# Attention and two feed-forwards: 768 plain and 1024 Strassen tokens instead of 896 and 896

## The chip, the cores and the metric

The kernel runs on one core of a Trainium2 chip. The metric is the device time of one execution in microseconds (us). PE is the tensor engine (matmul), PEld its weight loads, DVE the vector engine, ACT the scalar engine, POOL GpSimd, SP the engine that issues most DMAs.

## The reference

Multi-head attention with head mixing before and after the softmax, then two feed-forwards on the attention's output x (4 x 448 = 1792 tokens of 768):

```
scores = einsum('bhij,hg->bgij', q @ k.T / 8, w_pre)         # 4 batches, 12 heads, 448 x 448
attn   = softmax(scores); attn = einsum('bhij,hg->bgij', attn, w_post)
x      = attn @ v                                            # 1792 x 768
x      = (x @ w1) * (x @ w2) @ w3 @ w_out                    # 768 -> 1024 -> 1024 -> 768
h      = x @ w_in;  out = max(0.01 h, h) @ w_out2            # 768 -> 2048 -> 768
```

The inputs q, k, v are float32, the weights of the feed-forwards float64. The output is float32.

## The kernel before

Every product of the feed-forwards is made as three matmuls: each operand is split into a high part (rounded by ACT's copy, `hi_act`, L71) and a low part (the rest, by a DVE subtraction, `lo_dve`, L74), and high x high, high x low and low x high are added in PSUM. Weights arrive as 64-bit words and are converted on the chip (`converting`, L94): one copy on ACT (L99), four operations on DVE (L100 to L110), then the split. Three raw blocks can be in flight.

**Attention** (L117) is ordered by hand. Scores are made in chunks of 120, 120, 120 and 88 query columns; `pq` (L210) are the scores, evicted as `s`, rearranged by DMAs into `sr`, mixed across heads by `pm` (L277, premix), then softmax (`mx`, `e`, `sm`), weighing (`weigh`, L308 on ACT and L310 on POOL), `po` (L331, postmix), transposes `ap` on DVE, and `px` (L363), the product with v (`vs`). A table gives the step in which loads are issued; `at(max(g0//2-1, 2), "v", b)` (L449) loads batch 0's v in step 2, from ACT's queue. The result is stored in DRAM as `scr`: batches 0 and 1 already split into high and low, batches 2 and 3 whole.

**The drain.** While the last chunk of attention runs down, `seam()` (a generator in `first_half`) is advanced at fixed places: it loads x of the first 896 tokens (L711), converts the first w1 block and lets PE make the first 36 products `pm` (L541).

**First half** (`first_half`, L585): 896 tokens by plain products, 512 + 384 wide (`PARTS`). For each of 8 blocks of 128 hidden columns one w1 and one w2 product, beside which w_out and w3 are converted; then the fold (`pw`, L613: w3 times w_out, kept in DRAM as w34); then w34 and the w_in blocks (`pm`), and `second_product` (`po`, L555) with w_out2, in groups of FQ=4 w_in blocks.

**Second half** (`second_half`, L807): the other 896 tokens as two halves of 448, by a seven-product scheme of Strassen's kind (`seven`, L857; `pp`, L852) for w1/w2 and w_in, w34 by plain products, and `second_product` again. Converted blocks come back from DRAM (`kept_*`), sums of blocks from `sums_*`.

From the drain on, a scheduler that simulates the timeline sets the order of instructions on each engine. A DMA is issued on one of eight lanes (DMAHW0 to 7) taken in turn; it waits until the lane's earlier DMA has landed, and the issuing queue runs in order.

Of the kernel before, what the change touches and what calls it, by code (L numbers as in the profile page):

```python
# [8 lines left out]
F32 = mybir.dt.float32  # L9
# [13 lines left out]
def attention_moe_kernel(ctx: ExitStack, tc, qt, kt, vt, w_pre, w_post, w1, w2, w3t, w_out, w_in2, w_out2, out):  # L23
# [27 lines left out]
    while i0 < S:  # L51
# [4 lines left out]
    scr = [  # L56
        dram.tile([2, P, NPAIR, S], F32, name=f"scr_{b}") if b < 2 else dram.tile([P, NPAIR, S], F32, name=f"scr_{b}")
        for b in range(B)
    ]
# [57 lines left out]
    def attention(seam):  # L117
        with ExitStack() as es, ExitStack() as left:
# [229 lines left out]
            def av(b, c, p):  # L348
# [21 lines left out]
                def out():  # L370
                    hi, lo = (y[:, i, 2 * g:2 * g + 2, :ni] for i in range(2))
                    if b < 2:
                        hi_act(hi, px[:, :, :ni])
                    nc.scalar.copy(lo.bitcast(F32), px[:, :, :ni])
                    if b < 2:
                        nc.gpsimd.tensor_tensor(out=lo, in0=lo.bitcast(F32), in1=hi.bitcast(F32), op=ALU.subtract)
# [3 lines left out]
                if p == NPAIR - 1:  # L380
                    if b < 2:
                        later.extend((scr[b][i, :, :, c0:c0 + ni], y[:, i, :, :ni].bitcast(F32)) for i in range(2))
                    else:
                        later.append((scr[b][:, :, c0:c0 + ni], y[:, 1, :, :ni].bitcast(F32)))
# [132 lines left out]
    def moe():  # L517
        KM, KF, KF2 = DM // P, DF // P, DF2 // P
        T = 2 * S
        NT = T // P  # L520
# [3 lines left out]
        PARTS = ((0, 512), (512, T - 512))  # L524
# [21 lines left out]
        def second_product(g, wts, acc, s, f, beside=iter(())):  # L546

            for t in range(NT):
                for hf in range(2):
# [3 lines left out]
                    for m in range(FQ):  # L553
                        for j, (a, c) in enumerate(TERMS):
                            nc.tensor.matmul(  # L555
                                po, g[m][:, a, t * P:(t + 1) * P], wts[m][:, c, cs],
                                start=(m == 0 and j == 0), stop=(m == FQ - 1 and j == 2),
# [5 lines left out]
                if f + FQ == KF2:  # L563
                    r0 = s * T + t * P
                    nc.sync.dma_start(out=out[r0:r0 + P, :], in_=acc[:, t, :])
# [19 lines left out]
        def first_half():  # L585
            with ExitStack() as er:
# [4 lines left out]
                def wo_parts(kk):  # L591
# [5 lines left out]
                    if kk == 4:  # L597
                        t = ap.tile([P, NT, DM], F32R, tag="acc", name="wo")
                        extra = ap.tile([P, DM], F32R, tag="wx", name="wo")
                        for i in range(4, KF):  # L600
                            wos[i] = t[:, 2 * i - 8], (t[:, 2 * i - 7] if i < KF - 1 else extra)
# [97 lines left out]
                def seam():  # L699
# [42 lines left out]
                h0 = pool(es, "m_h0")  # L742
                xx = [x[:, kk] for kk in range(KM)]
# [37 lines left out]
                acc = ap.tile([P, NT, DM], F32, tag="acc", name="acc")  # L781
# [25 lines left out]
        def second_half():  # L807

            with ExitStack() as es:
# [3 lines left out]
                HALF = ((0, S), (S, S))  # L813

                def operand(name):
                    t = xo.tile([P, KH, 2, S], F32R, tag="xo", name=name, bufs=7)
# [31 lines left out]
                def product(w, i, b):  # L848
                    dst = bank([P, S], "pp")
# [8 lines left out]
                def seven(w, b, put_block):  # L858
# [3 lines left out]
                    def partial(tag, x, y):  # L862
                        u = tm.tile([P, S], F32, tag=tag, name=tag)
                        tt(u, x, y, ALU.add)
                        return u

                    x1 = product(w, A11, b11)
                    p1 = tm.tile([P, S], F32, tag="p1", name="p1")
                    nc.scalar.activation(out=p1, in_=x1, func=ACTF.Copy)
                    x5 = product(w, S1, t1)  # L870
                    put_block(0, 0, product(w, A12, b21), p1)
# [3 lines left out]
                    put_block(1, 1, x5, u3)  # L875
                    put_block(1, 0, product(w, A22, t4), u3)
# [199 lines left out]
```

## Time and profile before

| | us |
|---|---|
| runs (three) | 1226.17, 1231.8, 1974.27; median 1231.8 |
| profiled execution | 1224.22, span 1222.4 |
| PE busy | 1207.7 (99%) |
| DVE busy | 866.5 (71%) |
| ACT busy | 532.7 (44%) |
| POOL busy | 210.0 (17%) |
| DMA | 195.99 MB, mean 160 GB/s |

Busy shares are means over stages with different limits, so a change is read in the stage that it touches. A busy PE is not PE at its peak: what a matmul costs is read from a run of equal ones. Idle time of an engine that nothing waits for costs nothing. The granted clock of PE has a mean of 0.997 of full speed; its two levels are 1.2 and 2.4 GHz.

### The profile page before, as it was taken

What the parts mean: (1) busy time and instruction counts of PE and PEld (TensorE: products, weight loads), DVE (VectorE), ACT (ScalarE), POOL (GpSimd) and SP (SyncE); (2) the same over time, 40 slices, a digit from 0 to 9 for tenths busy, and PEclk for the clock granted to TensorE, in tenths of its full rate; (3) what the DMA queues carried; (4) which work ended last, traced back from release to release, by engine and by line L of the source; (5) the groups of instructions that cost most, each with busy time, mean ns of one, the idle gap of its engine ahead of it and who ended that gap; (6) DMA issues with size and microseconds to landing.
All of it is one profiled execution on the core that took longest, in us unless ns stands there. A gap on an engine that the chain in (4) does not pass through costs nothing.

```text
span 1222.4 us, 21998 instructions
## 1 busy us (share of the span) xinstructions
PE 1207.7 (99%) x8638; PEld 974.4 (80%) x8638; DVE 866.5 (71%) x1492; ACT 532.7 (44%) x1085; POOL 210.0 (17%) x163
## 2 busy tenths in 40 slices
PE   8899999999999999999999999999999999999998
PEld 5344444454468899998899999999999999999998
DVE  6677777777789988647795868567776657476572
ACT  3566666666655544322454333352233333323120
POOL 4566667656410000000000000000000000000000
PEclk9899999999999999999999999999999999999999
DMA  6767857856577665579664636063232221212012
GB/s 203 219 187 196 226 173 201 224 159 194 189 258 253 227 209 185 178 260 350 235 231 154 213 102 207 26 220 115 91 119 80 65 69 53 71 33 71 27 52 91
DMA packets 131007, 195.99 MB, mean 160 GB/s; under 512 B 26104, under 2 KB 110680, under 8 KB 130520
## 3 DMA queue, kind: packets, MB, share of 16 engines
q1 hardware_dynamic: 126768, 190.55, 48.7%
q10 hardware_dynamic: 4136, 4.04, 1.3%
q8 instruction: 68, 1.11, 0.4%
q14 instruction: 35, 0.29, 0.1%
HBM read 113.78 MB, written 42.07 MB: 128 GB/s over the span
## 4 chain that ended last, share of the span: by engine, by line
PE 93%; DMA 3%; ACT 1%; DVE 1%; issue 0%; ACTq 0%; POOL 0%; SPq 0%; POOLq 0%
PE pm L541 29%; PE po L555 19%; PE pp L852 17%; PE px L363 6%; PE po L331 6%; PE pw L613 6%; PE pq L210 5%; PE pm L277 5%; DMA sr<-s 2%; DMA vs<-in_v_dram 1%; ACT e L294 1%; DVE ap L346 1%; PE turn L264 0%; ACT s L218 0%; DVE mx L287 0%
## 5 line engine op out<-in xcount | busy, mean ns | idle before, releaser
L541 PE MATMUL pm<-x,ws 128*128 128x384 f32 (+1 forms) x1152 | 233.9, 364 | 0.0
L541 PEld LDWEIGHTS pm<-x,ws 128*128 128x128 f32 x1152 | 208.7, 188 | 24.5 <-issue 0.6
L310 POOL TENSOR_SCALAR e<-e,sm 128x448 f32<-128x448 f32 x128 | 184.9, 1457 | 140.9 <-DVE sm L304 123.7
L294 ACT ACTIVATE e<-pm,mx 128x448 f32<-128x448 f32 x180 | 111.8, 633 | 103.7 <-DVE mx L287 98.3
L346 DVE STREAM_TRANSPOSE ap<-po 128x512 f32<-128x512 f32 (+3 forms) x216 | 115.8, 594 | 33.4 <-PE po L331 33.3
L852 PE MATMUL pp<-t,w 128*128 128x448 f32 x576 | 124.5, 368 | 0.0
L555 PE MATMUL po<-ws,g 128*128 128x384 f32 x672 | 117.2, 334 | 0.0
L555 PE MATMUL po<-wo,g 128*128 128x384 f32 x672 | 117.1, 334 | 0.0
L852 PEld LDWEIGHTS pp<-t,w 128*128 128x128 f32 x576 | 108.1, 188 | 10.9
L555 PEld LDWEIGHTS po<-wo,g 128*128 128x128 f32 x672 | 116.6, 188 | 0.1
L555 PEld LDWEIGHTS po<-ws,g 128*128 128x128 f32 x672 | 116.6, 188 | 0.0
L363 PEld LDWEIGHTS px<-ap,vs 96*64 96x64 f32 (+1 forms) x1536 | 78.8, 138 | 33.5 <-ACT e L294 23.2
L287 DVE TENSOR_REDUCE mx<-pm 128x1 f32<-128x448 f32 x180 | 98.4, 602 | 2.7 <-PE pm L277 2.7
L99 ACT ACTIVATE wc<-wr 128x768 f32<-128x768 f32 (+1 forms) x72 | 61.7, 860 | 79.4 <-DMA wr<-in_moe_w_dram 30.6
L852 PE MATMUL pp<-b,w 128*128 128x448 f32 x432 | 95.5, 368 | 0.0
L562 DVE TENSOR_TENSOR acc<-po,acc 128x384 f32<-128x384 f32 x84 | 45.5, 553 | 68.7 <-PE po L555 68.4
L363 PE MATMUL px<-ap,vs 96*64 96x120 f32 (+3 forms) x1536 | 89.0, 268 | 3.9 <-DMA vs<-in_v_dram 3.7
L331 PE MATMUL po<-e,kpost 64*32 64x512 f32 (+1 forms) x1472 | 90.3, 592 | 1.3 <-POOL e L310 1.2
L218 ACT ACTIVATE s<-pq 120x448 f32<-120x448 f32 (+1 forms) x179 | 83.1, 563 | 18.4 <-PE pq L210 8.8
L852 PEld LDWEIGHTS pp<-b,w 128*128 128x128 f32 x432 | 81.0, 188 | 8.0
L210 PE MATMUL pq<-kl,ql 64*120 64x448 f32 (+1 forms) x384 | 87.0, 558 | 0.4 <-ACT s L218 0.4
L277 PE MATMUL pm<-sr,kpre 64*64 64x448 f32 x720 | 83.7, 550 | 2.7 <-DMA sr<-s 2.3
(101 smaller groups left out, 1486.2 us busy)
## 6 DMA issues: line engine op xcount, KB each, us to landing
sr<-s SPq DMA_DIRECT2D x121, 210.0 KB
wr<-in_moe_w_out_dram SPq DMA_DIRECT2D x24, 768.0 KB
wr<-in_moe_w_dram SPq DMA_DIRECT2D x16, 768.0 KB
wr<-in_moe_w_in_dram SPq DMA_DIRECT2D x16, 768.0 KB
wr<-in_moe_w_dram SPq DMA_DIRECT2D x16, 512.0 KB
sr<-s SPq DMA_DIRECT2D x44, 157.5 KB
kept_w<-wc SPq DMA_DIRECT2D x16, 384.0 KB
sa<-kept_w SPq DMA_DIRECT2D x16, 384.0 KB
```

Source lines behind the costliest of these rows:

```text
L210: nc.tensor.matmul(pq[e][:m], qls[b, c][rows, p, :m], kls[b, p // 2][rows, p % 2, :], start=True, stop=True)
L218: nc.scalar.activation(out=t[:m, e, :], in_=pq[e][:m], func=ACTF.Copy)
L277: nc.tensor.matmul(pms[ns[s % len(ns)]][half:half + Q], kpre[rows], sr[rows, 2 * t + g, :], start=True, stop=True,)
L287: nc.vector.tensor_reduce(out=mxs[n], in_=pms[n], axis=AX.X, op=ALU.max, negate=True)
L294: ends["act"] = nc.scalar.activation(out=e[:, i], in_=pms.pop(n), func=ACTF.Exp, bias=mxs.pop(n), scale=1.0, accum_out=sm[:, i:i + 1])
L310: ends["dve" if eng is nc.vector else "pool"] = eng.tensor_scalar(out=e[:, i], in0=e[:, i], scalar1=rc[:, i:i + 1], scalar2=None, op0=ALU.mult
L331: nc.tensor.matmul(po[g][32 * r:32 * (r + 1), :m], kpost[rows, x], e[rows, :m, JS[r]:JS[r] + P], start=True, stop=True,)
L346: ends["dve"] = nc.vector.transpose(out=dst, in_=po[g][:, i0:i1])
L363: nc.tensor.matmul(px[e * D:(e + 1) * D, r, :nw].rearrange("p (n i) -> p n i", i=HQ), vst[b][rows, jc, 2 * p + e, :], ap[rows, x, :ns, jc, ...
L541: nc.tensor.matmul(dst, wt[:, a, kk, :], x[kk][:, c, c0:c0 + w], start=(i == 0), stop=(i == len(steps) - 1))
L555: nc.tensor.matmul(po, g[m][:, a, t * P:(t + 1) * P], wts[m][:, c, cs], start=(m == 0 and j == 0), stop=(m == FQ - 1 and j == 2),)
L852: nc.tensor.matmul(dst, w[:, i, a, kk, :], b[:, kk, c, :], start=(kk == 0 and j == 0), stop=(kk == KH - 1 and j == 2),)
```

## The change

The plain half takes 768 tokens (384 + 384 wide), the Strassen half 1024 (two halves of 512). Attention stores the chunks that lie within the first 768 tokens split and all others whole, so 80 columns of batch 1 come whole into the first half and are split in the drain, by an ACT copy and a POOL subtraction. In the Strassen half the partial sums are made in place, the w34 blocks are staged in a `w7` tile, groups are two w_in blocks instead of four, and w_out2 is loaded after each seven products, ahead of the second w_in block's sums. Batch 0's v is loaded in step 0. The core of the diff:

```diff
+    T1, W = 768, 512
+    split_to = []
+    for b in range(B):
+        ends_ = [i0 + ni for i0, ni, _ in chunks if b * S + i0 + ni <= T1]
+        split_to.append(max(ends_, default=0))
...
-                at(max(g0 // 2 - 1, 2), "v", b)
+                at(max(g0 // 2 - 1, 0), "v", b)
...
-        PARTS = ((0, 512), (512, T - 512))
+        PARTS = ((0, T // 2), (T // 2, T // 2))
...
+        def pieces(t0, t1):
+            for b in range(t0 // S, (t1 - 1) // S + 1):
+                c0, c1 = max(t0 - b * S, 0), min(t1 - b * S, S)
+                n = min(max(split_to[b], c0), c1)
+                if n > c0:
+                    yield b * S + c0 - t0, scr[b][:, :, :, c0:n], True
+                if n < c1:
+                    yield b * S + n - t0, scf[b][:, :, n - split_to[b]:c1 - split_to[b]], False
...
-                    for n in range(2):
-                        for i in range(2):
-                            nc.sync.dma_start(out=x[:, :, i, n * S:(n + 1) * S].bitcast(F32), in_=scr[n][i])
+                    for c0, src, parted in pieces(0, T):
+                        c1 = c0 + src.shape[-1]
+                        if not parted:
+                            whole.append((c0, c1))
+                        for i in range(2) if parted else (1,):
+                            nc.sync.dma_start(
+                                out=x[:, :, i, c0:c1].bitcast(F32), in_=src[i] if parted else src
+                            )
                     fill()
                     yield
+                    for c0, c1 in whole:
+                        hi, lo = (x[:, :, i, c0:c1] for i in range(2))
+                        hi_act(hi, lo.bitcast(F32))
+                        nc.gpsimd.tensor_tensor(out=lo, in0=lo.bitcast(F32), in1=hi.bitcast(F32), op=ALU.subtract)
                     steps = converting(cv, loaded.pop(0), (KM, P))
...
+                T = 2 * W
+                FQ = 2
+                HALF = ((0, W), (W, W))
...
-                    u2 = partial("u2", product(w, S2, t2), p1)
-                    u4 = partial("u4", x5, u2)
-                    u3 = partial("u3", product(w, S3, t3), u2)
+                    tt(u, product(w, S2, t2), u, ALU.add)
+                    u4 = tm.tile([P, W], F32, tag="u4", name="u4")
+                    tt(u4, x5, u, ALU.add)
+                    tt(u, product(w, S3, t3), u, ALU.add)
```

**ACT and SP at the first v.** ACT's queue in the first steps of attention, before (`s` are evicted scores, `e` the softmax numerators, `vs` is batch 0's v; the brackets name what an instruction waits for):

```order
L294 ACTIVATE e,sm<-pm,mx 128x448 [waits DVE_49] x3
L218 ACTIVATE s<-pq 120x448 [waits DMAHW1_49,DMAHW0_49,PE_49]
L218 ACTIVATE s<-pq 120x448 [waits PE_49]
L218 ACTIVATE s<-pq 120x448 [waits DMAHW2_49,DMAHW3_49,PE_49,Activation_49]
L218 ACTIVATE s<-pq 120x448 [waits PE_49]
L189 DMA vs<-in_v_dram 96x3072 [waits DMAHW6_49]
L190 DMA vs<-in_v_dram 32x1536 [waits DMAHW0_49]
L294 ACTIVATE e,sm<-pm,mx 128x448 [waits DVE_49,Activation_49,Pool_49]
```

and with the change:

```order
L221 ACTIVATE s<-pq 120x448 [waits PE_49] x2
L221 ACTIVATE s<-pq 120x448 [waits DMAHW3_49,DMAHW2_49,PE_49]
L221 ACTIVATE s<-pq 120x448 [waits PE_49]
L192 DMA vs<-in_v_dram 96x3072 [waits DMAHW7_49]
L193 DMA vs<-in_v_dram 32x1536 [waits DMAHW1_49]
L297 ACTIVATE e,sm<-pm,mx 128x448 [waits DVE_49] x4
```

The load of v moves ahead of two groups of `e` and two of `s`, and takes lanes DMAHW7 and DMAHW1. On SP's queue the last parts of the second chunk's rows (`sr`, 5x12x448) and what follows stood, before:

```order
L243 DMA sr_106<-s 10x12x448 [waits DMAHW4_49,Activation_49]
L243 DMA sr_106<-s 5x12x448 [waits DMAHW5_49,Activation_49]
L243 DMA sr_106<-s 5x12x448 [waits DMAHW6_49]
L194 DMA ql<-in_q_dram 128x720 [waits DMAHW7_49,PE_49]
L243 DMA sr_107<-s 10x12x448 [waits DMAHW0_49,Activation_49,Pool_49]
```

and with the change:

```order
L246 DMA sr_107<-s 10x12x448 [waits DMAHW6_49,Activation_49]
L246 DMA sr_107<-s 5x12x448 [waits DMAHW7_49,Activation_49]
L246 DMA sr_107<-s 5x12x448 [waits DMAHW0_49]
L197 DMA ql<-in_q_dram 128x720 [waits DMAHW1_49,PE_49]
L246 DMA sr_108<-s 10x12x448 [waits DMAHW2_49,Activation_49,Pool_49]
```

The last part but one now waits for lane 7, on which v's transfer is the one before it.

**ACT in the drain.** Around the first weight copy (`wc<-wr`), before:

```order
L374 COPY y<-px 128x240 [waits DMAHW7_49,PE_49]
L258 DMA scr_60<-y 768x1x120
L294 ACTIVATE e,sm<-pm,mx 128x448 [waits DVE_49,Pool_49]
L294 ACTIVATE e,sm<-pm,mx 128x448 [waits DVE_49] x3
L99 ACTIVATE wc<-wr 128x768 [waits DMAHW5_49,DMAHW6_49,DMAHW1_49,DMAHW0_49]
L308 ACTIVATE e<-e,sm 128x448 [waits DVE_49,Activation_49]
L308 ACTIVATE e<-e,sm 128x448 [waits Activation_49] x2
L374 COPY y<-px 128x240 [waits PE_49]
```

and with the change:

```order
L377 COPY y<-px 128x240 [waits DMAHW5_49,PE_49]
L261 DMA scrf_61<-y 768x1x120
L297 ACTIVATE e,sm<-pm,mx 128x448 [waits DVE_49,Pool_49]
L297 ACTIVATE e,sm<-pm,mx 128x448 [waits DVE_49] x3
L74 ACTIVATE x<-x 128x6x80 [waits DMAHW3_49,DMAHW4_49,DMAHW2_49,DMAHW1_49]
L102 ACTIVATE wc<-wr 128x768 [waits DMAHW6_49,DMAHW1_49,DMAHW0_49]
L311 ACTIVATE e<-e,sm 128x448 [waits DVE_49,Activation_49]
L311 ACTIVATE e<-e,sm 128x448 [waits Activation_49] x2
L377 COPY y<-px 128x240 [waits PE_49]
```

The copy `x<-x` of the 80 whole columns is new and stands ahead of the weight copy and of the weighing (`e<-e,sm`).

**PE at the end of a group in the Strassen half.** The last group's passage from `pp` to `po` (`wo` are w_out2's blocks), before:

```order
L852 MATMUL pp_11424<-t4_9500,w7_11039 128x448 x9
L852 MATMUL pp_11439<-b22_9496,w7_11039 128x448 x9
L555 MATMUL po_11462<-wo_11348,g_11249 128x384 x3
L555 MATMUL po_11462<-wo_11352,g_11249 128x384 x3
L555 MATMUL po_11462<-wo_11454,g_11249 128x384 x3
L555 MATMUL po_11476<-wo_11348,g_11249 128x384 x3
L555 MATMUL po_11476<-wo_11352,g_11249 128x384 x3
L555 MATMUL po_11476<-wo_11454,g_11249 128x384 x3
L555 MATMUL po_11491<-wo_11348,g_11249 128x384 x3
```

and with the change:

```order
L878 MATMUL pp_11576<-t4_9380,w7_11134 128x512 x9
L878 MATMUL pp_11591<-b22_9376,w7_11134 128x512 x9
L568 MATMUL po_11614<-wo_11606,g_11509 128x384 x3
L568 MATMUL po_11622<-wo_11606,g_11509 128x384 x3
L568 MATMUL po_11631<-wo_11606,g_11509 128x384 x3
L568 MATMUL po_11639<-wo_11606,g_11509 128x384 x3
L568 MATMUL po_11648<-wo_11606,g_11509 128x384 x3
L568 MATMUL po_11656<-wo_11606,g_11509 128x384 x3
L568 MATMUL po_11665<-wo_11606,g_11509 128x384 x3
L568 MATMUL po_11614<-wo_11610,g_11509 128x384 x2
L568 MATMUL po_11622<-wo_11610,g_11509 128x384 x2
L568 MATMUL po_11631<-wo_11610,g_11509 128x384 x2
```

Before, one bank takes its four blocks in turn; now seven banks take the first block's three matmuls each before the second block's begin.

## Rows read from the trace of the kernel before

**Rows 1.** Windows: length, busy PE, PEld, DVE, ACT, POOL (instructions), granted clock, DMA share, GB/s.
```profile
341.20:365.70 24.50, 24.27 (x337) 18.20 (x337) 21.20 (x41) 13.54 (x31) 2.81 (x2) 1.00 0.73 242
365.70:460.30 94.60, 94.60 (x471) 84.93 (x470) 87.52 (x132) 48.33 (x72) 0.00 (x0) 1.00 0.68 226
608.00:638.00 30.00, 30.00 (x157) 27.77 (x156) 29.12 (x45) 17.37 (x28) 0.00 (x0) 1.00 0.67 211
630.40:805.00 174.60, 174.60 (x937) 165.66 (x937) 121.15 (x185) 66.52 (x105) 0.00 (x0) 1.00 0.41 140
805.00:842.00 37.00, 37.00 (x207) 36.27 (x207) 32.35 (x48) 17.55 (x23) 0.00 (x0) 1.00 0.68 238
998.00:1218.40 220.40, 220.40 (x1175) 210.60 (x1174) 137.06 (x220) 59.05 (x86) 0.00 (x0) 1.00 0.18 61
```

**Rows 2.** The chain of waits, PE after the drain: start us, us, line, count.
```profile
354.21 7.47 PE pm L541 x36
...
365.73 94.67 PE pm L541 x468
460.40 67.84 PE pw L613 x384
528.25 102.14 PE pm L541 x504
630.38 29.13 PE po L555 x168
...
834.11 104.16 PE pp L852 x504
938.27 59.52 PE pm L541 x288
```

**Rows 3.** PE's waits over the whole span: total us, times, longest.
```profile
PE px L363 <- DMA vs<-in_v_dram: 3.7, 1, 3.7
```

**Rows 4.** Windows around the first `px`: length, PE busy, granted clock, DMA share, GB/s.
```profile
49.75:53.45 3.70, 0.00 (x1) 0.81 0.83 167
53.45:58.45 5.00, 5.00 (x48) 0.50 0.67 219
58.45:62.00 3.55, 3.55 (x44) 0.94 0.85 237
```

**Rows 5.** The chain of waits, from 24 to 54 us.
```profile
24.34 3.67 DMA sr<-s
...
28.11 0.98 ACT s L218 x2
...
34.02 6.67 DMA sr<-s
...
40.72 12.60 DMA vs<-in_v_dram
```

**Rows 6.** Timeline of the drain: start us, us, instruction [idle before <-releaser].
```profile
336.90 0.94 ACT L99 ACTIVATE wc<-wr 128x768 f32<-128x768 f32 x1
...
339.41 1.79 ACT L308 ACTIVATE e<-e,sm 128x448 f32<-128x448 f32 x3 [1.57 <-DVE sm L304]
...
341.30 1.95 PE L331 MATMUL po<-e,kpost 64*32 64x512 f32 x32 [0.72 <-POOL e L310]
```

**Rows 7.** Timeline of SyncE's queue in the drain.
```profile
327.83 5.61 SPq L711 DMA_DIRECT2D x<-scr  x4
```

**Rows 8.** Windows in the drain: length, PE busy, granted clock, DMA share, GB/s.
```profile
330.00:348.00 18.00, 17.15 (x253) 1.00 1.06 383
348.00:352.00 4.00, 4.00 (x78) 1.00 0.51 188
```

**Rows 9.** Groups by form, DVE, 365.7 to 460.3: busy us, mean ns.
```profile
L74 DVE TENSOR_TENSOR h<-ht,h 128x512 fp32r<-128x512 f32 x6 | 4.1, 686 | 0.1
...
L74 DVE TENSOR_TENSOR h<-ht,h 128x384 fp32r<-128x384 f32 x6 | 3.3, 549 | 0.0
```

**Rows 10.** DVE's waits from 365 to 461 us.
```profile
DVE wc L100 <- ACT wc L99: 6.3, 8, 1.8
```

More of the change, by code (lines that the diff above doesn't have):

```diff
@@ L597, in wo_parts @@
                     if kk == 4:
[L598 to L601, printed above, removed]
+                        t = ap.tile([P, T // P, DM], F32R, tag="acc", name="wo")
+                        extra = xw.tile([P, 2, DM], F32R, name="wo")
+                        for i in range(4, KF - 1):
+                            wos[i] = t[:, 2 * i - 8], t[:, 2 * i - 7]
+                        wos[KF - 1] = extra[:, 0], extra[:, 1]
                     return wos[kk]
@@ L780, in first_half @@
                         nc.sync.dma_start(out=summed[kind, m0], in_=u)
-                acc = ap.tile([P, NT, DM], F32, tag="acc", name="acc")
+                acc = ap.tile([P, T // P, DM], F32, tag="acc", name="acc")
                 for f in range(0, KF2, FQ):
@@ L895, in second_half @@
                 for i, n, k in ((0, 0, 0), (5, 1, 0), (2, 1, 1), (1, 0, 1)):
-                    nc.sync.dma_start(out=low(x[i]), in_=scr[2 + n][:, k * KH:(k + 1) * KH])
+                    for c0, src, _ in pieces(T1 + n * W, T1 + (n + 1) * W):
+                        nc.sync.dma_start(
+                            out=low(x[i])[:, :, c0:c0 + src.shape[-1]], in_=src[:, k * KH:(k + 1) * KH]
+                        )
                 plan = []
@@ L921, in second_half, with w34_load @@
                     hp = pool(eh, "n_h")
-                    w3p = pool(eh, "n_w34a")
                     ht = hp.tile([P, KF, 2, T], F32R, tag="h", name="h")
                     h = [ht[:, kk] for kk in range(KF)]
-                    def w34_load(pool, m):
-                        t = pool.tile([P, 2, KF, P], F32R, tag="w34", name="w34")
+                    stage = []
+                    def w34_load(j, m):
+                        if not stage:
+                            stage.append(wb.tile([P, 7, 2, KH, P], F32R, tag="w7", name="w34", bufs=2))
+                        n = 2 * KF * P
+                        t = stage[0].rearrange("p i x k m -> p (i x k m)")[:, j % 2 * n:(j % 2 + 1) * n]
+                        t = t.rearrange("p (x k m) -> p x k m", x=2, k=KF)
                         nc.sync.dma_start(
@@ L941, in put_a @@
                             def put_a(i, n, p, u):
-                                a[i, n] = za.tile([P, S], F32, tag=f"a{i}{n}", name="a")
+                                a[i, n] = za.tile([P, W], F32, tag=f"a{i}{n}", name="a")
                                 tt(a[i, n], p, u, ALU.add)
                             def put_h(i, n, p, u):
-                                t = za.tile([P, S], F32, tag="ht", name="ht", bufs=2)
+                                t = tm.tile([P, W], F32, tag="gt", name="ht", bufs=2)
                                 tt(t, p, u, ALU.add)
                                 tt(t, t, a[i, n], ALU.mult)
-                                put(h[m + i * KF // 2], t, n * S, S)
+                                put(h[m + i * KF // 2], t, n * W, W)
+                            last = m == KF // 2 - 1
                             seven(ready.pop(0), x, put_a)
-                            ahead(2 if m < KF // 2 - 1 else 1)
+                            if last:
+                                for j in range(2):
+                                    w3[j] = w34_load(j, order[j])
+                            else:
+                                ahead(2)
                             seven(ready.pop(0), x, put_h)
-                            if m < KF // 2 - 1:
+                            if not last:
                                 ahead(2)
-                        w3 = {0: w34_load(w3p, 0)}
-                    w3q = pool(eh, "n_w34b")
                     swp[0] = pool(eh, "n_s2")
+                    ahead(1)
                     x2 = [operand(n) for n in names]
@@ L981, in second_half @@
                 swp[0] = pool(es, "n_s3")
-                acc = ac.tile([P, NT, DM], F32, tag="acc", name="acc")
+                acc = ac.tile([P, T // P, DM], F32, tag="acc", name="acc")
                 for f in range(0, KF2, FQ):
```

83 lines of the change are left out of this document (39 added, 44 removed).

## The prediction

> **What bounds the kernel now.** I first read the stages, window by window [rows 1]: from 341.2 us to the end TensorE (PE) is busy in practically every microsecond, while VectorE (DVE) has slack in some stages and almost none in others (87.5 of 94.6 us while the w1 and w2 blocks are converted, 29.1 of 30 us around 620 us). The reader should see two things: PE is the bound, and DVE stands close behind it in exactly the stages where plain products get cheaper. Second, the chain of waits gives PE's price list [rows 2]. Third, PE's own waits: the one large one is 3.7 us ahead of the first `px`, for batch 0's v [rows 3], and the clock around it [rows 4]. Last I read the two places where the change puts new waits into a queue: the start of v [rows 5] and the drain of attention, where the x of the first half is loaded [rows 6, 7, 8].
>
> The profiled execution took 1224.2 us (span 1222.4); the median of the three runs shown is 1231.8. The sum below is made against 1224.2.
>
> **PE's columns.** 384 columns cost 29.13/168 = 173.4 ns and 67.84/384 = 176.7 ns; I take 175.0. 448 columns cost 104.16/504 = 59.52/288 = 206.7 ns. The plain products mix 512 and 384 at 94.67/468 = 202.3 ns, so 512 costs 2 x 202.3 - 175.0 = 229.6 ns [rows 2]. Plain: 36+468+504 and three blocks of 144, 1440 matmuls in all, go from 202.3 to 175.0: -39.3 us. Strassen: 2 x 504 `pp` and 288 `pm` go from 206.7 to 229.6: 1296 x 22.9 = +29.7 us. The `po` matmuls do not change in number: 96 leave the first half (-16.7) and 96 join the second (+16.7). Columns alone: **-9.7 us**. With 173.4 for 384 (231.2 for 512) it is -9.9, with 176.7 (227.9) it is -9.4, so this term is nearly certain, provided PE is fed.
>
> What speaks against it is a rule of the Trainium skill ("TensorE: Matmul & The Clock Gate", section Back-to-back issue gap): a warm matmul follows another after N/2.4 + 2.5 ns, the same price for each column. By that page 384, 448 and 512 columns would cost 162.5, 189.2 and 215.8 ns, and the columns would bring only 1440 x -26.7 + 1296 x 26.7 = -3.8 us. The trace does not agree: its 448 row lies 17.5 ns over the formula and its 384 row 11 to 14 ns, which is why the rows make 448 a dear width. The sum goes by the rows.
>
> **v two steps sooner.** Gain: the 3.70 us wait goes [rows 3]. With it goes what followed: while PE idled the granted clock fell to its lower level (0.50, 1.2 GHz), and it stayed there for the next 5.0 us of matmuls, in which half the work of the upper level was done: another 2.5 us [rows 4]. Together -6.2. Cost: the two transfers, issued at 40.72 before, now stand in ACT's queue behind the evictions that end at 29.09; with the 12.60 us that they took [rows 5], v would land at about 41.7. They take DMA lanes out of their turn: the last but one part of sr1 on SyncE's queue waits for DMAHW7, v's lane, and SP runs in order, so the last part, ql and the parts of sr2 queue behind it. In the kernel before this last part was issued at 34.02 and landed at 40.69, and PE's `pm` (premix) ran on it. Now it would be issued about 42.5 and land 3.67 us later (the quickest such landing in these rows; SP's queue has run empty by then), at about 46.2, or after 6.67 us again, at 49.2 [rows 5]. PE idles 46.2 - 40.7 = 5.5 us there, and the clock should fall again (+2.5). Net 5.5 + 2.5 - 6.2 = **+1.8**, between -6.2 (v lands before 34 us, nobody waits) and +4.8 (6.67 us).
>
> **The drain of attention.** The first half's tokens are now batch 0 and 320 columns of batch 1, of which 80 are kept whole and have to be split on the spot: one ACT copy and one POOL subtraction. ACT's copy `x<-x` waits for the x loads and stands ahead of the first weight copy and of the weighing of the last softmax group, which the next `po` needs. Before, this weight copy started at 336.90 without a wait, the weighing at 339.41, `po` at 341.30 [rows 6], and PE has no gap afterwards. The x loads were four of 128 x 6 x 448 floats, 5376 KB, issued from 327.83 on [rows 7], and the DMA engines are saturated at 383 GB/s up to 348 [rows 8]. Now they are (2 x 688 + 80) columns in five loads, 4368 KB, 0.81 of it. If the old ones ended at 348, 20.2 us after the first issue, the new ones end after 0.81 of that, at about 344; if they had the rate to themselves, 4.47 MB would take 11.7 us and end before 340. ACT would wait from 336.9 to 344, 7.1 us, then copy 480 elements a row (the weight copy's 768 took 0.94, so some 0.7), and everything behind is 8 us late: **+8** for PE (3 to 10), and after such an idle stretch the lower clock for some 5 us of work, **+2.5**.
>
> **Up to the fold.** Two paths reach the fold's start at 460.40. PE: 504 matmuls, 27.3 ns less each, -13.8, plus 8 plus 2.5: 457.1. Conversions: from 341.2 to 460.3 DVE has 21.2 + 87.5 = 108.7 us of work [rows 1], of which 12 operations shrink from 512 to 384 columns (0.686 to 0.549 us [rows 9]): 107.1. Started 8 us later, with the 6.3 us in which DVE waited for ACT's copy [rows 10], it ends at 349.2 + 107.1 + 6.3 = 462.6. Without any wait it would be 456.3, with the idle share of before (9%) 467. The later path counts: **+2.2** (-3.3 to +6.6) instead of -13.8. So the late drain and the conversions overlap: only the later of the two is paid.
>
> **Second stage of the plain half** (528 to 630): -13.8 by columns. In its last 22 us DVE has nothing left to give (29.12 of 30 [rows 1]), so 13.5% of 22, 3.0 us, is not had: **-10.8** (-13.8 to -8). The `pm` of the three later groups: **-11.8**; DVE is busy 121 of 174.6 us from 630 to 805 [rows 1] and converts ahead during `po`, which covers it; without that cover they would lose as the second stage does, 3 us. First half's `po`: **-16.7**.
>
> **Strassen half.** Columns +29.7, `po` +16.7. Groups of two: eight passages from `pp` to `po` instead of four. Each ends with an addition, the leaky maximum, ACT's copy and the low part, about 2.8 us by the 512 row, hidden behind the last product (2.1 us) and the m=0 matmuls that PE now takes first (21 x 173 ns = 3.6 us). The additions into acc go from 42 to 112, 70 x 0.549 = 38 us more for DVE, which had 137 of 220 us there [rows 1]; with wider rows it comes to about 184 of 249, 74%. I take **+2** (0 to +8). In-place partial sums, the w34 staging in the w7 tile and w_out2 ahead of w_in's second block I cost at nothing: PE never waited there, and DVE and the DMA engines have slack (DMA share 0.18 after 998). The entry at 805 to 842 is tight: 32.4 of 37 us for DVE, and 512-wide sums make it up to 36.9 where PE now passes in 32.8; its bound is 0 to +4.
>
> Sum: +1.8 + 2.2 - 10.8 - 11.8 - 16.7 + 29.7 + 16.7 + 2 = **+13.1**, so 1224.2 + 13.1 = **1237 us**.
>
> **Rivals.** *Columns decide.* The x loads land by 337, conversions keep up, v's wait is simply gone: -9.7 - 6.2 = -15.9, 1208 us. For it: PE never waited for DVE after 341. Against it: ACT's queue order, and 92% DVE in the first stage. Chance 0.20, with a spread of 1200 to 1220.
> *The passages stall (slower).* If the put of the second block's first half comes later than the 5.7 us of cover (2.1 + 3.6), because DVE is behind with accumulations, PE waits at every passage. At 3.6 us each, eight make +29 instead of +2: 1264 us. It decides from the point where DVE's backlog at the end of a group exceeds 3 us. For it: 70 added operations fall in the `po` before. Against it: 26% idle. Chance 0.13.
> *Width is priced by the column.* From the 448 row, 384 would cost 177.2 and 512 236.2: Strassen +38.2, later w_in blocks and second stage 2.2 less gain: +10.7 on the sum, 1248 us. The rows speak against it (the mix of 512 and 384 cost 202.3, not 206.7). Chance 0.10. The section of the Trainium skill named above prices by the column too, from a lower level.
> My forecast keeps 0.57, by itself 1226 to 1247: the unknown ends of v, drain and first stage.
>
> Two per cent, 25 us, is about what a measurement of this kernel can tell from no change. Range 1211 to 1251: it leaves out about half of the first rival and most of the second. Faster by over 2% only in the lower half of the first rival, 0.08; slower in the second rival, 0.12; within 2%, 0.80.
>
> **What would show it.** No PE wait for vs, but one for sr near 41 us and a lower clock behind it; an ACT wait ahead of `x<-x` that ends on the x load near 344, and a PE gap of about 8 us at the `po` after it; the fold starting near 463 with PE waits on DVE's `ws` or `wo` before it; 384-wide matmuls at 175 ns and 512-wide at 230; no PE gap at `po` after 850. A `pp` over 235 ns, a PE that never waits in the w1/w2 stage, or x landed by 337 would make the prediction wrong.

## The result, and the profile after

The changed kernel takes 1241.9 us (median of four runs, 1240.65 to 1246.49) against 1230.7 us of the kernel before beside it: a ratio of 1.0124 (95% interval 1.0098 to 1.0150). One slow run of the kernel before, 1974.3 us, counts in its median and not in the ratio, so the two medians as they stand would give 1.009. The change is slower, clear of noise, and within 2%. The forecast was 1237 us, with a range of 1211 to 1251. It took 25 us as about what such a measurement can tell; the interval is 3 us either way. The profiled execution took 1241.8 us:

```profile
span 1240.0 us, 22093 instructions
...
PE 1204.7 (97%) x8638; PEld 967.3 (78%) x8638; DVE 909.7 (73%) x1556; ACT 530.2 (43%) x1080; POOL 207.6 (17%) x158
```

The span grew by 17.6 us, while PE's busy time fell by 3.0 us, although more of it ran at the lower clock (mean granted clock 0.987, before 0.997): the columns' gain is there, and the waits are more than it. PE's waits over the whole span (total, times, longest):

```profile
PE po L334 <- ACT e L311: 9.2, 1, 9.2
PE pw L626 <- ACT ws L74: 3.4, 1, 3.4
PE pm L544 <- DVE ws L77: 3.3, 5, 1.3
PE pm L280 <- DMA sr<-s: 2.9, 3, 1.6
PE pm L280 <- ACT s L221: 2.2, 1, 2.2
PE pq L213 <- ACT s L221: 2.1, 1, 2.1
PE po L568 <- DVE gt L580: 2.0, 1, 2.0
```

Of before's 3.7 us for vs [rows 3] nothing is left. New are one wait of 9.2 us in the drain of attention, waits for converted weights up to the fold (`pm` and `pw` on `ws`), waits near 31 and 41 us for evictions, and waits of `po` for `g`, the leaky maximum of the w_in products, near 1000 us. The chain of waits gives the new prices, to be held against [rows 2]:

```profile
467.65 68.88 PE pw L626 x380
536.53 88.16 PE pm L544 x504
624.70 24.97 PE po L568 x144
649.66 24.96 PE pm L544 x144
...
915.26 65.29 PE pm L544 x288
...
1019.32 14.32 PE pp L878 x63
1033.65 16.66 PE po L568 x96
```

504 plain matmuls take 88.16 us where they took 102.14, a group's `po` and `pm` 24.97 us each instead of 29.13 and 29.07. So 384 columns cost 173.4 to 174.9 ns. 512 columns cost 65.29/288 = 226.7 ns and 14.32/63 = 227.3 ns. In the last stage, from the second group on, a passage from `pp` to `po` costs nothing: 96 `po` in 16.66 us are 173.5 ns each.

Held against before by the start of the same matmuls, the 17.6 us come about like this:

| stretch | before, us | after, us | difference |
|---|---|---|---|
| up to the drain's `px` | 338.6 | 339.7 | +1.1 |
| from there to the next `px` | 6.4 | 16.9 | +10.5 |
| on to the w1/w2 stage, with the first 36 `pm` | 20.7 | 19.3 | -1.3 |
| w1/w2 stage, 468 `pm`, to the fold | 94.6 | 90.4 | -4.2 |
| fold, 384 `pw` | 67.8 | 70.1 | +2.2 |
| second stage, 504 `pm` | 102.1 | 88.2 | -14.0 |
| groups of the plain half | 203.7 | 174.8 | -29.0 |
| `pp` block, 504 | 104.2 | 115.8 | +11.6 |
| w34, 288 `pm` | 59.5 | 65.3 | +5.8 |
| last stage | 224.8 | 259.6 | +34.8 |

**The drain.** In the timeline ACT's copy `x<-x` starts after 7.63 us of idling, when the x loads have landed; the row names the load of `wr`, but the copy reads x alone, and whole_first below shows that it was x's last load. The weighing and then `po` follow:

```profile
345.73 0.60 ACT L74 ACTIVATE x<-x 128x480 fp32r<-128x480 f32 x1 [7.63 <-DMA wr<-in_moe_w_dram]
...
349.01 1.78 ACT L311 ACTIVATE e<-e,sm 128x448 f32<-128x448 f32 x3 [1.90 <-DVE sm L307]
...
350.89 1.96 PE L334 MATMUL po<-e,kpost 64*32 64x512 f32 x16 [9.23 <-ACT e L311]
```

The windows of PE there (length, busy, granted clock, DMA share, GB/s) show the second half of the price:

```profile
341.00:346.00 5.00, 0.66 (x13) 0.92 1.13 356
346.00:351.00 5.00, 0.11 (x8) 0.50 0.32 127
351.00:356.00 5.00, 5.00 (x42) 0.56 0.00 0
356.00:361.00 5.00, 5.00 (x80) 1.00 0.02 5
```

PE idles, the clock goes to 0.50, the 5 us of work after the gap are done at 0.56, and from 356 us on it is 1.00 again.

**The first passage.** `po` of the first group begins at 994.66 us and stops three times:

```profile
994.66 1.58 PE L568 MATMUL po<-wo,g 128*128 128x384 f32 x8
...
997.21 1.51 PE L568 MATMUL po<-wo,g 128*128 128x384 f32 x7 [0.98 <-DVE g L77]
...
999.51 0.56 DVE L580 TENSOR_TENSOR sw<-sw,w 128x384 f32<-128x384 f32 x1 [1.75 <-DMA sw<-kept_wi]
999.99 1.28 DVE L580 TENSOR_TENSOR gt<-pp,p 128x512 f32<-128x512 f32 x2
...
1000.73 2.29 PE L568 MATMUL po<-wo,g 128*128 128x384 f32 x6 [2.00 <-DVE gt L580]
...
1004.12 2.29 PE L568 MATMUL po<-wo,g 128*128 128x384 f32 x6 [1.11 <-ACT g L74]
```

The seven products take sums of a pair of w_in blocks, and each block and sum split into a high and a low part; the groups that follow have theirs prepared here. DVE stands 1.75 us before such a sum (`sw`) whose load has not landed, and `gt`, the addition that `po` waits for, is behind it in DVE's queue. The first block of 96 `po` lasts 24.5 us instead of 16.7: 4.2 us are waits and 3.6 us work at the lower clock (0.86 over the block).

### The profile page after: what moved, and what is told of

Read it like the earlier page. It is cut to its first block, busy times and chain, and to the rows that moved or that the text cites. A ratio compares the mean times of both kernels' runs of the same rounds, so it can differ in the third digit from the quotient of the medians.

```text
span 1240.0 us, 22093 instructions
## 1 busy us (share of the span) xinstructions
PE 1204.7 (97%) x8638; PEld 967.3 (78%) x8638; DVE 909.7 (73%) x1556; ACT 530.2 (43%) x1080; POOL 207.6 (17%) x158
## 4 chain that ended last, share of the span: by engine, by line
PE 82%; DVE 7%; DMA 6%; ACT 2%; issue 2%; SPq 1%; ACTq 0%; DVEq 0%
PE pm L544 18%; PE pp L878 17%; PE po L568 16%; PE po L334 6%; PE px L366 6%; PE pq L213 6%; PE pw L626 6%; PE pm L280 5%; DMA wr<-in_moe_w_dram 3%; DMA sr<-s 2%; DVE wc L113 1%; DVE wc L109 1%; SPq L728 1%; ACT wc L102 1%; DMA b<-scrf 1%
## 5 line engine op out<-in xcount | busy, mean ns | idle before, releaser
L544 PE MATMUL pm<-x,ws 128*128 128x384 f32 x1152 | 203.3, 335 | 3.4 <-DVE ws L77 3.3
L544 PEld LDWEIGHTS pm<-x,ws 128*128 128x128 f32 x1152 | 199.4, 188 | 6.6 <-DVE ws L77 5.2
L568 PE MATMUL po<-wo,g 128*128 128x384 f32 x768 | 138.2, 339 | 4.2 <-DVE gt L580 2.0
L568 PEld LDWEIGHTS po<-wo,g 128*128 128x128 f32 x768 | 135.7, 191 | 6.3 <-DVE gt L580 2.3
L349 DVE STREAM_TRANSPOSE ap<-po 128x512 f32<-128x512 f32 (+3 forms) x216 | 116.0, 594 | 29.9 <-PE po L334 29.6
L878 PE MATMUL pp<-t,w 128*128 128x512 f32 x576 | 136.7, 389 | 0.0
L878 PE MATMUL pp<-b,w 128*128 128x512 f32 x432 | 106.0, 390 | 0.8 <-DVE b L77 0.5
L568 PE MATMUL po<-ws,g 128*128 128x384 f32 x576 | 100.5, 334 | 0.0
L568 PEld LDWEIGHTS po<-ws,g 128*128 128x128 f32 x576 | 99.9, 188 | 0.0
L575 DVE TENSOR_TENSOR acc<-po,acc 128x384 f32<-128x384 f32 x148 | 75.5, 550 | 29.4 <-PE po L568 29.2
```

The source lines that it names most:

```text
L349: ends["dve"] = nc.vector.transpose(out=dst, in_=po[g][:, i0:i1])
L544: nc.tensor.matmul(dst, wt[:, a, kk, :], x[kk][:, c, c0:c0 + w], start=(i == 0), stop=(i == len(steps) - 1))
L568: nc.tensor.matmul(po, g[m][:, a, t * P:(t + 1) * P], wts[m][:, c, cs], start=(m == 0 and j == 0), stop=(m == len(g) - 1 and j == 2),)
L878: nc.tensor.matmul(dst, w[:, i, a, kk, :], b[:, kk, c, :], start=(kk == 0 and j == 0), stop=(kk == KH - 1 and j == 2),)
```

## The experiments

All ratios are to the kernel before, run beside each kernel on the same chip. The other columns are read from the starts of matmuls in each trace: the longest PE wait in the drain, the w1/w2 stage up to the fold, the block of 504 `pp`, and the first block of `po` in the last stage (96 matmuls, or the number in brackets), with PE's waits in that block and its granted clock. The last two have to be read together: a block is long by its waits and by what the lower clock takes after them.

| kernel | ratio (95%) | drain | w1/w2 stage | `pp` block | first `po` | waits in it | clock |
|---|---|---|---|---|---|---|---|
| before | 1 | 0.7 | 94.6 | 104.2 | 29.1 (168) | 0.0 | 1.00 |
| changed | 1.0124 (1.0098 to 1.0150) | 9.2 | 90.4 | 115.8 | 24.5 | 4.2 | 0.86 |
| whole_first | 1.0078 (1.0061 to 1.0095) | 1.5 | 90.0 | 115.4 | 26.2 | 6.0 | 0.87 |
| v_step2 | 1.0185 (1.0166 to 1.0203) | 10.6 | 90.4 | 116.2 | 25.6 | 4.3 | 0.80 |
| rest_at_896 | 1.0061 (1.0044 to 1.0078) | 0.7 | 94.6 | 104.2 | 20.2 (84) | 3.1 | 0.92 |
| wo_two_tiles | 1.0127 (1.0109 to 1.0146) | 8.7 | 89.8 | 115.8 | 22.2 | 4.9 | 1.00 |
| whole_first_v2 | 1.0076 (1.0046 to 1.0106) | 1.5 | 91.7 | 114.9 | 26.3 | 6.1 | 0.87 |
| whole_first_raw4 | 1.0040 (1.0013 to 1.0067) | 1.5 | 87.3 | 115.6 | 24.5 | 4.4 | 0.86 |
| rest_896_ahead2 | 1.0040 (1.0021 to 1.0058) | 0.7 | 94.6 | 104.2 | 19.7 (84) | 3.1 | 0.91 |
| whole_first_presum | 1.0035 (1.0018 to 1.0053) | 1.5 | 90.3 | 116.0 | 21.9 | 4.6 | 1.00 |
| raw4_presum | 1.0054 (1.0032 to 1.0076) | 1.5 | 88.7 | 116.5 | 24.3 | 4.4 | 0.86 |
| parted_one | 1.0053 (1.0033 to 1.0073) | 1.5 | 89.8 | 122.2 | 18.2 | 1.3 | 1.00 |
| parted_two | 1.0059 (1.0042 to 1.0077) | 1.5 | 88.9 | 121.1 | 16.7 | 0.0 | 1.00 |
| all_together | 0.9979 (0.9962 to 0.9997) | 0.7 | 88.9 | 115.0 | 16.7 | 0.0 | 1.00 |

**The drain: whole_first.**

```diff
-                    for c0, src, parted in pieces(0, T):
+                    for c0, src, parted in sorted(pieces(0, T), key=lambda p: p[2]):
```

> The changed kernel, but the load of the 80 whole columns is the first of the five x loads instead of the last. Theory (the drain is held up by the last x load, on which ACT's copy x<-x waits): the whole columns land near 335 us, ACT does not wait, the 9.2 us gap ahead of po and the lower clock behind it (2.0 us) go, po starts near 341.5 us. Conversions start 9 us sooner too, so the fold starts near 457 us instead of 466.3, and the time falls by about 9 to 10 us, to some 1232 us. Rival (the conversions are paced by the weight loads alone, so the drain's gap is hidden behind them): the gap goes, but the fold starts at 463 us or later and the time falls by less than 4 us.

```profile
336.53 0.61 ACT L74 ACTIVATE x<-x 128x480 fp32r<-128x480 f32 x1
...
341.71 1.87 PE L334 MATMUL po<-e,kpost 64*32 64x512 f32 x25 [1.50 <-ACT e L311]
```

ACT's copy now runs at 336.53 us, `po` follows at 341.71 and not at 350.89; of its wait 1.5 us remain, for the copy and the subtraction themselves. The fold starts at 455.0 instead of 466.3 us. The span is 9.3 us shorter; the ratio falls by 0.0046, which is 5.6 us, give or take some 4 by the two intervals. The rival, that the conversions hide the gap, falls: they start with the drain, since the same ACT queue feeds them.

**v: v_step2 and whole_first_v2.**

```diff
-                at(max(g0 // 2 - 1, 0), "v", b)
+                at(max(g0 // 2 - 1, 2), "v", b)
```

> The changed kernel with batch 0's v loaded in step 2 again, as before. Theory (the early v trades one wait for others: 3.7 us and 5 us of lower clock at px against waits of pq and pm near 31 and 41 us with the lower clock): the wait for vs of 3.7 us is back, those near 31 and 41 us go, and the time stays within 2 us of the changed kernel's. Rival (moving v brought its full 6 us): the time rises by 5 to 6 us. Other rival (moving v cost several us): it falls by 4 us or more.

> The kernel with the whole columns loaded first, and batch 0's v loaded in step 2 as in the kernel before. The profiles reached the drain's px at 338.3 to 344.8 us with the early v and at 338.6 to 340.1 with the late one, while the times put the late v 4 to 6 us behind. Theory (early v is neutral, the start spreads by itself): within 3 us of whole_first, ratio to the kernel before 1.006 to 1.010. Rival (early v brings 4 to 6 us): ratio 1.011 to 1.013.

In v_step2 the wait for vs is back (2.7 us), and those for evictions near 31 and 41 us are gone but for 0.4 us, as expected, but the ratio rises by 0.006, as the rival had it. The pair with the drain mended says otherwise: 1.0078 with the early v, 1.0076 with the late one, although the late v costs what it cost before and more:

```profile
PE px L366 <- DMA vs<-in_v_dram: 5.1, 2, 4.5
```

The profiles agree with the pair: PE reaches the drain's `px` at 338.6 us in the kernel before, at 340.1 and 341.3 in the two kernels with the late v, and at 337.0 to 344.8 in those with the early one. v's step is worth nothing that these runs can tell. Why v_step2 is slower stays open; its trace puts most of 3.2 us at places far from v (the drain's wait 1.4 us longer, the first passage 1.1, and that by the clock, 0.80 for 0.86, with the same waits).

**The rest of the change alone: rest_at_896.**

```diff
-    T1, W = 768, 512
+    T1, W = 896, 448
...
-        PARTS = ((0, T // 2), (T // 2, T // 2))
+        PARTS = ((0, 512), (512, T - 512))
...
```

> All of the change but the split: 896 plain tokens, 512 and 384 wide, and 896 Strassen tokens in halves of 448, so no column is split in the drain. Early v, partial sums in place, groups of two and the order of loads stay as changed. Theory: no gap in the drain, the plain half as in the kernel before; only the first passage from pp to po in the last stage waits (4.2 us of gaps and the lower clock, 7.9 us in the changed kernel, some less at 448 columns) and the start moves by 1 us: 1230 to 1235 us on the scale of the kernel before's 1224 to 1231, that is 5 to 9 us above it. Rival (groups of two cost nothing by themselves; the wider rows make DVE late there): within 2 us of the kernel before.

The plain half is before's to 0.1 us and so is the `pp` block. The 8.4 us by which its span exceeds before's are 2.8 us at the start and 5.7 us in the first passage (20.2 us for 84 `po` of 14.6). So the passage is no matter of width: groups of two and the order of loads bring it along, at 448 columns too.

**The first passage: wo_two_tiles, rest_896_ahead2, whole_first_presum.**

```diff
-                            t = so.tile([P, 2, DM], F32R, tag="ws", name="wo", bufs=4)
+                            t = so.tile([P, 2, DM], F32R, tag="ws", name="wo", bufs=2)
```

> The changed kernel with two w_out2 tiles in the Strassen half's last stage instead of four, so the second group's two w_out2 blocks cannot be split ahead of the first group's first passage. Theory (DVE is late at the first passage because it splits four w_out2 blocks in 980 to 995 us): 2 x 0.95 us of DVE work leaves that place, the gaps of 4.2 us there shrink to 2 us or less, the first po block takes 20 to 22 us instead of 24.5, and the time falls by 2 to 5 us if the later passages stay covered. Rival (DVE stands in its queue behind the weight sums that wait for their load until 999.4 us): the gaps stay and the time is the same within 1 us.

The block shrinks by 2.3 us to 22.2, just outside the theory's 20 to 22, but not by its waits: they are 4.9 us where they were 4.2, and the block is shorter because the clock stayed at 1.00 in it. The ratio is the same. The theory falls; the four splits of w_out2 are not shown to cost anything here, and the rival's gaps stay.

```diff
...
-                    ahead(1)
                     x2 = [operand(n) for n in names]
...
+                        if j == 1:
+                            ahead(2)
```

The lines that give w34 two tiles of its own are left out.

> The kernel with the rest of the change at 896 tokens, but w34 staged in two tiles of its own and both first w_in blocks prepared while w34 is multiplied, as in the kernel before (the narrower halves leave the room). Theory (the first passage waits because the second w_in block's sums and parts are made during the first seven products): the first po block takes 14.6 to 15.5 us instead of 20.2, and the time falls by 4 to 6 us, to a ratio of 1.001 to 1.003. Rival (groups of two are too short for the put at the first passage): it still takes 18 us or more.

The theory falls as it was put: 19.7 us are left of 20.2. With the second pair out of the way it is the third one's sums and splits that stand ahead of the last `g`, and now in ACT's queue:

```profile
1019.14 0.62 DVE L1023 SCALAR_TENSOR_TENSOR gt<-gt 128x448 f32<-128x448 f32 x1
...
1019.51 1.48 ACT L74 ACTIVATE w<-sw 128x1536 fp32r<-128x1536 f32 x1
...
1020.89 1.25 ACT L573 ACTIVATE acc<-po 128x384 f32<-128x384 f32 x3
...
1022.00 0.61 ACT L74 ACTIVATE g<-gt 128x448 fp32r<-128x448 f32 x1
...
1022.66 1.50 PE L568 MATMUL po<-wo,g 128*128 128x384 f32 x7 [3.06 <-ACT g L74]
```

DVE is done with `gt` at 1019.76, but ACT first splits the third pair's sums (`w<-sw`) and evicts three `po`, and copies the high part of `g` only at 1022.00; on that copy PE's 3.06 us end. In the first group alone ACT evicts `po` (L573); in the later ones DVE does. The third pair is loaded from 1013.15 us on, in the midst of the passage.

```diff
-            for kind in ("w1", "w2") for m in range(KF // 2)
+            for kind, ms in (("w1", range(KF // 2)), ("w2", range(KF // 2)), ("wi", (2, 4))) for m in ms
...
+                        if f + FQ == KF2 and m < 2:
+                            four_sums(u, *(a[:, i] for i in range(4)))
+                            nc.sync.dma_start(out=summed["wi", 2 * m + 2], in_=u)
```

> The kernel with the whole columns loaded first, and the sums of the second and third w_in block pairs made in the plain half's last w_in phase and kept in DRAM, as those of w1 and w2 are. It moves 8 DVE operations of 0.47 us and the wait for their loads out of the first passage. Theory (DVE's queue, full and standing behind those sums, makes the first passage late): the first po block takes 19 to 22 us instead of 26.2, and the time falls by 4 to 7 us, to a ratio of 1.002 to 1.005. Rival (the splits of the blocks, 3.1 us each, do it): it stays above 24 us and the time within 2 us of whole_first.

The block falls by 4.4 us to 21.9 and the ratio by 0.0043, as the theory has it. But only 1.4 us of the 4.4 are waits (4.6 us for 6.0); the other 3.0 are the clock, which stayed at 1.00. And what is left of the waits ends on ACT:

```profile
993.92 1.16 ACT L74 ACTIVATE w<-w 128x1152 fp32r<-128x1152 f32 x1 [6.70 <-DMA w<-kept_wi]
994.99 1.13 ACT L74 ACTIVATE g<-gt 128x512 fp32r<-128x512 f32 x2
...
996.17 4.98 PE L568 MATMUL po<-wo,g 128*128 128x384 f32 x27 [3.30 <-ACT g L74]
```

ACT stands 6.70 us before a split of the third pair whose load has not landed, with the copies of `g` behind it. So it is not DVE's queue alone: a pair's preparation stands ahead of `g` in both queues.

**The w1/w2 stage: whole_first_raw4.**

```diff
-                    while pos[0] < len(plan) and pos[0] < pos[1] + 3 and (folded or plan[pos[0]][0] != "w34"):
+                    while pos[0] < len(plan) and pos[0] < pos[1] + 4 and (folded or plan[pos[0]][0] != "w34"):
...
-                    wp = pool(es, "m_raw", 3)
+                    wp = pool(es, "m_raw", 4)
```

> The kernel with the whole columns loaded first, and four raw weight buffers in flight instead of three. In whole_first the w1/w2 stage takes 90.0 us to the fold where its columns at 173.4 ns would take 81.2. Theory (DVE, 93% busy there, is the limit): the stage and the fold's start stay within 1.5 us and the time too. Rival (the weight loads are: ACT's first copy waits for them, and a fourth buffer lets them start sooner): the fold starts 3 to 6 us sooner, and the time falls by as much.

It lies between the two: 2.7 us off the stage. That is more than the buffer brings on the whole: the six kernels with three buffers and 384-wide products take 89.8 to 91.7 us, the five with four 87.3 to 89.8, 1.7 us apart by their means. ACT's waits for raw weights in whole_first, from 365 to 455 us:

```profile
ACT wc L102 <- DMA wr<-in_moe_w_dram: 24.0, 13, 3.5
ACT wc L102 <- DMA wr<-in_moe_w_out_dram: 7.7, 4, 3.2
```

and with four buffers:

```profile
ACT wc L102 <- DMA wr<-in_moe_w_out_dram: 6.5, 3, 2.3
```

DVE (third busy column) from 365 to 450 us, first whole_first, then with four buffers:

```profile
365.00:450.00 85.00, 80.88 (x458) 78.59 (x455) 79.59 (x119) 43.03 (x65) 0.00 (x0) 1.00 0.72 233
```

```profile
365.00:450.00 85.00, 82.86 (x468) 80.51 (x466) 81.52 (x124) 45.23 (x65) 0.00 (x0) 1.00 0.71 236
```

The loads were late by turns, and DVE used that as it could; with them in time DVE is 96% busy and the stage still takes 6.1 us more than its columns' 81.2. The first limit is the loads; that the second and larger one is DVE is read from its 96%, and no run here takes work off DVE in this stage to show it.

**Together: raw4_presum, parted_one, parted_two, all_together.**

The edits of whole_first_raw4 and whole_first_presum in one kernel:

> Whole columns first, four raw buffers and the sums of the second and third w_in pairs made beforehand, together. Theory (three separate places, so the gains add): ratio 1.0078 - 0.0038 - 0.0043 = 0.9997 to the kernel before (0.998 to 1.002), first po block about 21.9 us. Rival (what one brings the other takes, since DVE is behind in both places): 1.003 or more.

The gains do not add: the passage is back at 24.3 us, the ratio at 1.0054. But the waits in that block are those of whole_first_presum (4.4 us for 4.6), and of whole_first_raw4, where the sums were not made beforehand (4.4); what is back is the lower clock (0.86 for 1.00). So the ratio is the rival's, its reason is not shown, and the sums made beforehand are worth between 0 and 1.4 us of waits.

```diff
+                                    hi_act(hi, t)
+                                    lo_dve(lo, t, hi)
...
+                    if kind == "wi" and m0 in parted7:
+                        nc.sync.dma_start(out=ws.bitcast(F32), in_=parted7[m0])
+                        return w
```

> As raw4_presum, but of the second w_in pair all seven block operands are also split into high and low parts in the plain half's last w_in phase and kept so in DRAM; in the last stage they are loaded and nothing of that pair is left for DVE and ACT. It takes 3.1 us of DVE work more out of the first passage. Theory (DVE's queue makes the first passage late): the first po block takes 17.5 to 20 us, 2 to 4 us off raw4_presum. Rival (the wait is the put's own chain, three ACT and DVE steps behind each other): it stays at 21 to 22 us.

> As parted_one, with the third pair kept split as well. Theory (DVE's queue makes the first passage late): the first po block takes 16.7 to 17.5 us, its columns alone, and the ratio to the kernel before is 0.993 to 0.997. Rival (the second pair had its place in the queue ahead of the put, the third has it behind): no gain over parted_one. If the extra splits do not fit into the slack of the last w_in phase (DVE 16.9 of 25 us busy), PE waits near 765 us and the gain is lost there.

```profile
780.66 9.93 DMA b<-scrf
...
977.83 14.28 PE pp L902 x63
992.11 16.66 PE po L568 x96
1008.78 14.32 PE pp L902 x63
```

With one pair kept split the first `po` block takes 18.2 us, with two 16.7, its columns alone: nothing is left of the wait. That settles the passage as far as the cause is the preparation of the second and third pairs; since it leaves ACT's queue together with DVE's, these runs do not part the two. The ratio misses its forecast (1.0059, not 0.993 to 0.997): the second half's operands are now loaded late. The first `b<-scrf` is issued at 776.0 us instead of 764.0 in whole_first, behind the stores of the splits, the last of them at 765.6, and behind w1's loads in SP's queue, and the `pp` block pays 5.7 us (121.1 against 115.4). Whether the tiles that the splits hold play a part too is not shown. The wait was moved, not removed.

all_together therefore makes the splits in a tile of `h` that is free by then, one pair a group earlier, and also splits x's 80 columns only after attention's last weighing.

```diff
+                def part_block(m0):
+                    t = h0.tile([P, 2, 2, 4, KH * P], F32R, tag="h", name="parts")
...
+                    if f == KF2 - 2 * FQ:
+                        part_block(2)
...
```

> The split at 768 and 1024 with what the runs point to: whole columns loaded first and split only after the last weighing of attention, four raw buffers, and the second and third w_in pairs kept split in DRAM, made in h's free tile during the third group and the last w_in phase of the plain half, so the second half's loads do not wait for them as in parted_two (pp block 121.1 us instead of 115.4). Theory (each wait was a queue's order, not a price of the split): no gap in the drain (1.5 us in whole_first), first po block 16.7 us, pp block 115 to 116 us; against parted_two's profile 5.5 + 1.5 us less, a ratio to the kernel before of 0.998 to 1.002. Rival (the slack is used up, DVE work put off from one place makes PE wait at the next): 1.004 or more, with a new wait in the third group or at the second half's entry.

```profile
span 1216.2 us, 22090 instructions
...
PE 1196.2 (98%) x8638; PEld 963.0 (79%) x8638; DVE 908.5 (75%) x1556; ACT 533.9 (44%) x1080; POOL 207.3 (17%) x158
```

The chain of waits from the second half's entry on:

```profile
784.13 18.02 PE pp L906 x79
802.92 96.22 PE pp L906 x423
...
978.69 16.66 PE po L568 x96
```

Drain 0.7 us, `pp` block 115.0, first `po` block 16.7: span 1216.2 us, 24 us under the changed kernel's and 6 under before's. Those 6 us flatter it: the profiled run was the fastest of twelve (1218.0, median 1224.3 against 1225.5), and its clock stayed at 1.00 through the fold (69.2 us), where raw4_presum and the parted ones, with the same waits, had 0.95 to 0.98 (70.7 to 71.8 us). By the times it is the one version that is below both, 0.9979 (0.9962 to 0.9997) of the kernel before: a gain of 0.2%, far under the 2% that count as clear.

## Why the prediction was right, step by step

- **Columns, -9.7.** Right in kind, a little mis-sized: 512 columns were taken at 229.6 ns by subtraction and cost 227.0, 384 at 175.0 and cost 173.4 to 174.9. The Strassen half's columns brought 11.6 + 5.8 + 10.3 = +27.7 instead of +29.7 (0.8 us of the 11.6 are waits at the half's entry, for which the forecast had 0 to +4); the plain half's, where PE was not held up, 14.0 + 12.3 us for 936 matmuls, 28.1 ns each instead of 27.3. The price by the column would have made the `pp` block and w34 dearer by 792 x 29.5 ns = 23.4 us; they rose by 17.4. By the formula for a single gap in the Trainium skill ("TensorE: Matmul & The Clock Gate", Back-to-back issue gap) going from 448 to 512 columns would add an estimated 26.7 ns. These runs show 20.3.
- **v, +1.8.** Half of the mechanism came as written: SP waits 5.5 us for v's lane, and the last part of sr is issued when v has landed, at 41.8 us:

```profile
41.77 8.06 DMA sr<-s
```

  But for sr PE waits 1.3 us there and not 5.5; its larger waits are two for ACT's evictions, 2.1 us near 31 and 2.2 us near 41, which the forecast did not have (a wait of 1.5 us near 29 us stands in whole_first_v2 too, with the late v). So the sum at the drain, +1.1, is near the forecast in part by luck. Unforeseen was also that the start spreads by several us from kernel to kernel, more than the term, and that the clock falls after shorter waits too (below).
- **Drain, +8 and +2.5.** Measured +8.5 (9.2 for 0.7) and +2.0. whole_first shows that it was the load's place in the order.
- **Up to the fold, +2.2 for the columns' -13.8.** The overlap of drain and conversions was right, the wait sized a little low: with v's 1.1 us the fold should start at 463.7 and starts at 466.3, the last 3.4 us of it PE's wait for the fold's first `ws`. The clock falls behind that wait (0.73 from 466.3 to 470 us, 0.86 to 475), which with a second wait of 0.4 us makes the fold 2.2 us longer. whole_first_raw4 adds that late loads have a share in it.
- **Second stage, -10.8.** Wrong in size: -14.0, the whole of the columns. DVE's 97% around 620 us was not work that PE waits for: in the changed kernel DVE does 68.0 us in this stage where it did 76.3, and PE has no wait there. What that work was for is not shown.
- **Later groups, -11.8 and -16.7.** Measured -12.3 and -16.6.
- **Passages, +2.** This is the step that failed: no PE gap was to come at `po` after 850 us, and 4.2 us of them came near 1000. Seven passages cost nothing, the first cost +7.8 (the waits and 3.6 of lower clock), which lies inside the bound of 0 to +8, but not by the path forecast: a late `g`, as in the rival, but at one place only and not for accumulations, which DVE does not have in the first group. I read the cover of a passage in the steady state and not the first, where the sums and splits of the second and third pairs stand ahead of `g` in the queues of DVE and ACT, in part before loads that have not landed. The order of loads was costed at nothing for the mean slack of DVE and the DMA engines; the mean of a stage says nothing about its first ten us.

The errors partly cancelled: second stage -3.2, columns -2.0, v -0.7, passage +5.8, fold +2.6 and +2.2. 13.1 us were forecast, the spans differ by 17.6. That the time came out within 5 us of the forecast is in part luck: the terms missed by 5.9 us one way and 10.6 the other.

## What to carry to other kernels

A gain on the bounding engine is worth what the engines behind it leave: read, stage by stage, how busy they are, and what their queues hold at the stage's start. When a load is split into several, put first the piece that an in-order queue waits for. And when a wait has been removed by doing its work earlier, look at what now stands behind that work in the queues. Before a shorter stage is put down to an edit, part its waits from its clock.

## What was not expected of the hardware

The granted clock of PE fell after waits of about 2 us as well. In the changed kernel's start (windows: length, PE busy, granted clock, DMA share, GB/s):

```profile
28.00:31.00 3.00, 1.27 (x6) 1.00 0.59 192
31.00:35.00 4.00, 3.60 (x14) 0.52 0.96 248
35.00:38.00 3.00, 3.00 (x32) 0.51 0.91 216
42.00:46.00 4.00, 4.00 (x24) 0.65 0.81 246
```

PE waited 2.1 us before 31.4 us and 2.2 us before 41.3 us, and the matmuls after each ran at its lower level for most of the time: 0.52 and 0.51 from 31 to 38 us, which took 3.4 us on top of the first wait, and 0.65 from 42 to 46, 1.4 us on top of the second. But the length of a wait does not settle it. In the first passage whole_first_presum and wo_two_tiles had waits of 3.3 and 3.0 us and kept a clock of 1.00, while raw4_presum, after one of 3.4 us, ran the 6.7 us of work behind it at 0.58. What decides stays open here; it is worth about 3 us to a kernel, as much as most of the edits above.

And 448 columns are a dear width: 206.7 ns lie 6.5 ns above the middle of the 173.4 ns of 384 and the 227.0 ns of 512. Over 1296 matmuls those 6.5 ns are 8.4 us, the larger part of what PE's sum gains when 128 tokens move into a wider Strassen half. There are also 9216 columns fewer (64 less in 1440 matmuls, 64 more in 1296), some 4 us at the 0.42 ns a column that lie between those two widths.
